# Scores from two 32 bit parts: the two heads of a pair in two 64-row halves, one PSUM bank for each score tile

## The chip, the core and the metric

The kernel runs on one core of a Trainium2 chip. The core has a matrix engine (TensorE; PE in the profile, PEld for its weight loads), a vector engine (DVE), a scalar engine (ACT), GpSimd (POOL) and a queue engine (SP) that issues most DMA transfers. Matmuls take their operands from SBUF and write to PSUM, which has eight banks; a bank holds 128 x 512 numbers of 32 bits. The engines run side by side and wait for each other on semaphores; each works through its own instructions in order.

The metric is the time of one execution on the device in microseconds, as the median of several runs.

## The reference

A block of a transformer with an attention that also has a compressive memory, 2048 positions, width 512, 32 heads of 16, and a feed-forward layer of width 1792; its input is modulated by a condition vector. The sequence is cut into four segments of 512. Cut to what matters here, the attention of a segment and head is

```python
logits = jnp.einsum("bhqd,bhkd->bhqk", qs, ks) * scale + mask     # causal
p = _softmax(logits, axis=-1)
a_dot = jnp.einsum("bhqk,bhkd->bhqd", p, vs)
o = g * a_mem + (1.0 - g) * a_dot
```

with `q = x @ wq` and so on, and `a_mem` read from the sums of earlier segments. Then come `o @ wo`, a residual, a layer norm, and the feed-forward layer with GELU. All of it is wanted at 32 bit accuracy, so the kernel splits operands of matmuls into parts and adds the products of the parts.

## The kernel before

**Stages.** The first is the projections: for each segment, layer norm, transposes, q, k, v (`proj`, `v_rows`), and the memory. The second is the attention loop with the output projection, the residual and the second layer norm woven in. The third is the feed-forward layer. In the trace they lie at about 0 to 180 us, 180 to 470 us and from there to the end.

**q and k in three parts.** `proj` (L483) makes a 128 x 512 tile of q or k in PSUM for eight heads. ACT rounds it to bfloat16 (the first part), DVE subtracts (`r1`, L497), ACT rounds the rest (second part, L508), and POOL subtracts again (third part, L509). `store` (L477) writes the parts to DRAM tiles QD and KD, which have six copies: for every product of parts that is wanted there is one place c, with one part of q in QD and one part of k in KD (`TERMS`, L162). Since a head has 16 numbers, six places make 96 rows. `load_stacks` (L172) brings the 96 rows of four heads back as `qst` and `kst` tiles of 128 x 4 x 512; one matmul over 96 rows then gives the score of a head to the accuracy of six products.

**Units of the loop.** Q counts groups of four heads within a segment (32 in all), P pairs of heads (64; P = 2Q and 2Q + 1). There are four pairs of stack tiles (`NK`). Two kinds of work make the softmax:

- S (`s_part`, L619) computes scores with query rows on the partitions, for a block i of 128 queries against the 128 (i + 1) keys that it may see, so 512, 384, 256 or 128 columns. DVE takes the negated maximum of each row: `masked_max` (L611) adds the causal mask and reduces in one instruction; for some blocks of 128 columns (`PRM['m']`: block 0 of each pair with Q below 14) a matmul adds the mask in PSUM and one `s_max` reduces both heads. S of pair P + 4 runs while T of pair P does (`LEAD`).
- T (`st_part`, L699) computes the transposed scores, key rows on the partitions, for a block j of 128 keys against 512 - 128 j queries. Three more rows (96 to 98) of the stacks hold the maxima, cut into three bfloat16 parts in `qst` against ones in `kst`, so that the matmul of 99 rows also subtracts the maximum (`st_mm`, L691). ACT takes the exponential into `pt` tiles, and POOL zeroes what the mask forbids (`causal`).

**The way of the maxima.** `m_rows` (POOL) cuts them into parts, `m_put` (PE) transposes them by a matmul with an identity into the bank of the pv tile, ACT copies them to `ms`, and `m_send` moves them by DMA into rows 96 to 98 of `qst`; the DMA is issued by SP for Q below 13 and by ACT from there on.

**The rest of the loop.** `pv_part` (L724) multiplies the exponentials of the four heads of Q with V, 32 columns for each head, so four column strips of the array; a column of ones in V gives the denominator. Then come the division (`den`, `rb_in`, `mix`) through DRAM tiles, and the output projection (`wo_part`, L815: three matmuls of 512 columns).

**The order.** It is written out by hand. The string `ORDER` is run once for each Q: `S1` is part 1 of S, `T2` part 2 of T (a token's first occurrence is for pair 2Q, its second for 2Q + 1), and `c0` to `c19` are positions at which other work is put, by numbers in `PRM`: work at 20Q + n runs at cn of Q's own turn. So `'pv'` puts the first part of pv of Q (key block 0) at 20Q + 31, which is c11 of the turn of Q + 1, and the others at c16 to c18; `'mrows'`, `'mput'` and `'msl'` place the way of the maxima; `'stacks'` (-65) places `load_stacks` at c15 four turns ahead; `'wo'` places two wo parts in a turn. Six PSUM banks (`att`) are handed out in turn to S and T; one bank is for pv and one (`mm`) for wo.

Of the kernel before, what the change touches and what calls it, by code (L numbers as in the profile page):

```python
# [25 lines left out]
ORDER = ('S1 c0 T2 T3 T2 c1 S2 c2 S3 T3 S3 c3 c4 c5 T5 S0 c6 c7 T0 c8 c9 '  # L26
         'T1 T4 S2 c10 c11 T5 S1 c12 T4 S0 c13 T0 c14 T1 c15 c16 c17 c18 c19')
# [3 lines left out]
 'mrows': -26,  # L31
 'mput': [-19, -17],
# [14 lines left out]
 'wo': [[20 * i + o for i in range(8) for o in (2, 5)]] * 2 + [[20 * i + o for i in range(4) for o in (2, 5, 8, 14)]],  # L47
# [54 lines left out]
def block_kernel(ctx: ExitStack, tc: tile.TileContext, x, wq, wk, wv, wo, betaq, betam,  # L102
# [9 lines left out]
    identb = per.tile([128, 128], BF16, name="identb")  # L112
# [59 lines left out]
    def load_stacks(Q):  # L172
        s, g, t = Q // 8, (Q // 2) % 4, Q % 2
        for st, dd in ((kst[Q % NK], KD), (qst[Q % NK], QD)):
            sp.dma_start(st[:96], dd[s][g].rearrange("c r e n -> (c r) e n")[:, 4 * t:4 * t + 4, :])
# [7 lines left out]
    v.tensor_copy(identb, ident)  # L183
# [18 lines left out]
    with ExitStack() as pa:  # L202
# [274 lines left out]
        def store(parts, nm, dd):  # L477
            rows = dd.rearrange("c r e n -> (r e) c n")
            for t, c in zip(parts, TERMS[nm]):
                d = rows[:, c]  # L480
                sp.dma_start(d, t.unsqueeze(1).to_broadcast([128, d.shape[1], 512]))

        def proj(s, nm, g):  # L483
# [7 lines left out]
            parts = [sa.tile([128, 512], BF16, tag=f"qk{i}", bufs=3, name=f"{nm}{i}{s}_{g}") for i in range(3)]  # L491
            r1 = sa.tile([128, 512], F32, tag="qkr", bufs=2, name=f"{nm}r{s}_{g}")
# [4 lines left out]
            v.tensor_tensor(out=r1, in0=ps, in1=parts[0], op=ALU.subtract)  # L497
# [10 lines left out]
            act.activation(parts[1], r1, AF.Copy)  # L508
            pool.tensor_tensor(out=parts[2], in0=r1, in1=parts[1], op=ALU.subtract)  # L509
# [74 lines left out]
    with ExitStack() as pb:  # L584
# [8 lines left out]
        nmt = [sb.tile([128, 8, 16], F32, name=f"nm{i}", bufs=1) for i in range(4)]  # L593
        for t in nmt:
            v.memset(t[:, 3:], 0.0)
# [838 lines left out]
```

## Time and profile before

| what | before |
| --- | --- |
| median of 3 runs | 785.87 us (785.84 to 789.34) |
| span of the profiled execution, first to last instruction | 783.4 us |
| the profiled execution's own time | not given apart from its span |
| PE busy | 767.0 us, 98% |
| DVE busy | 557.4 us, 71% |
| ACT busy | 470.6 us, 60% |
| granted TensorE clock | 1.000 |

In a view that groups instructions, a row names line, engine, operation, output <- inputs, shapes and count; after the first bar stand the busy time in us and the mean length of one in ns, after the second the engine's idle time ahead of them in us and who ended it. A timeline row has start and length in us. A stretch has its bounds, its length, and the busy time of PE, PEld, DVE, ACT and POOL, then the granted clock, the DMA engines' mean share and GB/s. Matmuls are pipelined: a length includes the time until the last result is written, so busy PE isn't PE at its peak.

### The profile page before, as it was taken

How to read it: one execution, taken by the hardware profiler on the slowest of the kernel's cores; microseconds unless marked ns; L12 is line 12 of the kernel's file. 1: busy time of each engine (PE TensorE's matmuls, PEld its weight loads, DVE VectorE, ACT ScalarE, POOL GpSimd, SP SyncE). 2: the span in 40 equal slices, each digit the busy share in tenths (PEclk: the TensorE clock that was granted, in tenths of full speed). 3: DMA queues.
4: the chain of work that ended last, by engine and by line, in shares of the span. 5: the costliest groups of instructions: out<-in, count | busy, mean ns of one | idle time of the engine just before them, and what ended most of it. 6: DMA issues, size and time to landing. Idle time of an engine off the chain costs nothing.

```text
span 783.4 us, 14172 instructions
## 1 busy us (share of the span) xinstructions
PE 767.0 (98%) x4549; PEld 529.0 (68%) x4549; DVE 557.4 (71%) x1540; ACT 470.6 (60%) x910; POOL 315.1 (40%) x535
## 2 busy tenths in 40 slices
PE   9999999999999999999999899999999999999998
PEld 4877776877444444455455457788878888888887
DVE  6687677548988888888987798868569764432424
ACT  4465546364888877777778676667644446652221
POOL 1256467261468556665795671243000404300000
PEclk9999999999999999999999999999999999999999
DMA  9596956487465586777677755595676624545543
GB/s 340 182 314 218 312 177 225 160 265 266 137 181 171 163 216 196 214 208 237 183 192 222 206 158 155 187 313 180 202 233 208 191 95 162 172 148 165 173 127 115
DMA packets 108819, 156.09 MB, mean 199 GB/s; under 512 B 16325, under 2 KB 55621, under 8 KB 108745
## 3 DMA queue, kind: packets, MB, share of 16 engines
q1 hardware_dynamic: 106911, 153.39, 62.4%
q10 hardware_dynamic: 1833, 1.81, 0.7%
q8 instruction: 35, 0.57, 0.3%
q14 instruction: 40, 0.32, 0.1%
HBM read 93.95 MB, written 60.83 MB: 198 GB/s over the span
## 4 chain that ended last, share of the span: by engine, by line
PE 48%; DVE 5%; DMA 5%; ACT 3%; issue 2%; POOL 2%; ACTq 0%; DVEq 0%; POOLq 0%
PE bx L1081 8%; PE bx L1351 5%; PE bv L1081 5%; PE by L1351 4%; PE bv L1351 4%; PE att L693 4%; PE pv L733 4%; PE att L606 4%; PE mm L821 3%; DMA qst<-ms 3%; PE spare L1351 2%; PE by L1081 2%; PE mm L1351 1%; ACT pt L708 1%; DMA s<-GD 1%
## 5 line engine op out<-in xcount | busy, mean ns | idle before, releaser
L613 DVE CUSTOM_DVE_ANT_0 dump<-att,maskb 128x384 bf16<-128x384 f32 (+1 forms) x456 | 208.3, 511 | 36.4 <-PE att L606 16.7
L708 ACT ACTIVATE pt<-att 128x384 f32<-128x384 f32 (+1 forms) x256 | 126.0, 545 | 33.7 <-PE att L693 16.6
L696 POOL TENSOR_SCALAR_AFFINE_SELECT pt<-pt 128x256 f32<-128x256 f32 x256 | 104.1, 422 | 68.4 <-ACT pt L708 55.7
L693 PE MATMUL att<-qst,kst 99*128 99x256 bf16 (+3 forms) x512 | 107.7, 300 | 4.2 <-DMA qst<-ms 1.8
L606 PE MATMUL att<-kst,qst 96*128 96x384 bf16 (+1 forms) x456 | 104.2, 310 | 0.8 <-DVE nm L613 0.7
L693 PEld LDWEIGHTS <-kst 99*128 99x128 bf16 x512 | 44.6, 97 | 72.6 <-issue 39.6
L865 POOL TENSOR_TENSOR wb<-wa 128x256 f32<-128x256 f32 x24 | 19.7, 821 | 153.1 <-DMA wa<-in_w 84.4
L733 PE MATMUL pv<-pt,V 128*32 128x512 f32 (+1 forms) x992 | 79.6, 439 | 0.0
L719 ACT ACTIVATE pt<-att 128x256 f32<-128x256 f32 (+1 forms) x128 | 62.4, 493 | 13.8 <-PE att L693 13.6
L136 DVE TENSOR_TENSOR gl<-s,gh 128x512 fp32r<-128x512 f32 x34 | 24.0, 707 | 42.4 <-ACT gh L133 42.4
L733 PEld LDWEIGHTS pv<-pt,V 128*32 128x32 f32 x992 | 25.9, 109 | 36.3 <-issue 30.5
L606 PEld LDWEIGHTS <-qst 96*128 96x128 bf16 x456 | 36.8, 98 | 19.2 <-issue 13.7
L133 ACT ACTIVATE gh<-s 128x512 fp32r<-128x512 f32 x34 | 21.3, 628 | 47.1 <-PE spare L1351 17.6
L1086 ACT ACTIVATE s<-s,b1t 128x512 f32<-128x512 f32 x42 | 30.3, 721 | 21.6 <-DVE s L1090 21.6
L1090 DVE TENSOR_TENSOR s<-bv,s 128x512 f32<-128x512 f32 x28 | 19.2, 687 | 30.4 <-PE bv L1081 21.2
L613 DVE DVE_READ_ACCUMULATOR2_ANT nm<- 128x1 f32 x456 | 37.7, 83 | 0.0
L509 POOL TENSOR_TENSOR q<-qr,q 128x512 bf16<-128x512 f32 x16 | 18.7, 1166 | 28.1 <-ACT q L508 27.9
L136 DVE TENSOR_TENSOR w1ml<-s,w1mh 128x512 fp32r<-128x512 f32 x18 | 13.0, 720 | 21.9 <-ACT w1mh L133 21.9
L500 POOL TENSOR_SCALAR qp<-qp 128x512 f32<-128x512 f32 x12 | 18.7, 1562 | 24.2 <-ACT qp L495 24.2
L661 POOL TENSOR_TENSOR nm<-nm 128x16 f32<-128x16 f32 x64 | 13.9, 217 | 34.3 <-DVE nm L613 31.2
L133 ACT ACTIVATE w1mh<-s 128x512 fp32r<-128x512 f32 x18 | 11.3, 628 | 25.9 <-PE spare L1351 11.6
L313 PE MATMUL q<-Ahl,wqh 128*128 128x512 f32 x64 | 26.0, 406 | 0.3 <-DVE Ahl L136 0.2
(362 smaller groups left out, 2043.5 us busy)
## 6 DMA issues: line engine op xcount, KB each, us to landing
GD<-s SPq DMA_DIRECT2D x56, 256.0 KB
s<-GD SPq DMA_DIRECT2D x52, 256.0 KB
kst<-KD SPq DMA_DIRECT2D x32, 384.0 KB
qst<-QD SPq DMA_DIRECT2D x32, 384.0 KB
TD<-ts SPq DMA_DIRECT2D x32, 256.0 KB
xt<-X2D SPq DMA_DIRECT2D x28, 256.0 KB
wa<-in_w SPq DMA_DIRECT2D x28, 256.0 KB
QD<-q SPq DMA_DIRECT2D x16, 384.0 KB
```

The source lines that it names most:

```text
L133: act.activation(hi, src, AF.Copy)
L136: lo_eng.tensor_tensor(out=lo, in0=src, in1=hi.bitcast(F32), op=ALU.subtract)
L606: pe.matmul(ps, q_of(P, h, i), k_of(P, h, 128 * (i + 1)), start=True, stop=True)
L613: v.tensor_tensor_reduce(out=dump[n_dump[0] % 2][:, :n], in0=src, in1=maskb[:, 512 - n:], scale=-1.0, scalar=-4 * NEG, op0=ALU.add, op1=AL ...
L693: pe.matmul(ps, k[:99, e, 128 * j:128 * j + 128], q[:99, e, 128 * j:512], start=True, stop=True)
L696: pool.affine_select(out=t, in_=t, pattern=pattern, compare_op=ALU.is_ge, fill=0.0, base=0, channel_multiplier=-1)
L708: act.activation(pt[:, h, :], ps[:, :n], AF.Exp, scale=0.25)
L719: act.activation(pt, pv_, AF.Exp, scale=0.25)
L733: pe.matmul(ps[32 * c:32 * c + 32, lo:hi], V[4 * s + j][:, VW * hd:VW * hd + 32], pt[:, c % 2, lo - o:hi - o], start=start, stop=stop)
L1081: pe.matmul(ps, a[:, i, k, :], b[k], start=start and k == 0 and c == 0, stop=k == 1 and c == 2, skip_group_check=not start)
L1086: act.activation(dst, src, AF.Gelu_apprx_tanh, bias=b1t[:, f:f + 1])
L1351: pe.matmul(ps, a[:, c], w[:, lo:hi], start=(f == 0 and i == 0), stop=(last and i == 2))
```

## The change

q and k are cut into two parts of 32 bits (the type that TensorE takes as fp32r), not three of bfloat16; ACT's second rounding and POOL's subtraction go. Three products of parts are kept instead of six, so a head needs 48 rows. The two heads of a pair then lie one above the other: head 0 in rows 0 to 47 and head 1 in rows 64 to 111 of the stack tiles, which are 128 x 2 x 512 numbers of 32 bits. The maxima are cut into two parts in rows 48 and 49 of each half, and T's matmuls have 50 rows.

S and T are now units of one head and one bank. Unit a is the block of 512 columns, b that of 384, c the blocks of 256 and 128 together in one bank. In `ORDER`, `Sa0` is unit a of S for head 0 of the first pair of the turn, `Tc3` unit c of T for head 1 of the second. Units of the two halves follow each other in turn. All maxima are masked maxima; the matmul that added the mask goes. The `pt` tiles are one for each unit, with three buffers for a and four for b and c.

`m_rows`, `m_put` and the wo parts get other positions, and every `m_send` is two transfers from SP. `load_stacks` is four transfers instead of two.

The core of the diff:

```diff
-ORDER = ('S1 c0 T2 T3 T2 c1 S2 c2 S3 T3 S3 c3 c4 c5 T5 S0 c6 c7 T0 c8 c9 '
-         'T1 T4 S2 c10 c11 T5 S1 c12 T4 S0 c13 T0 c14 T1 c15 c16 c17 c18 c19')
+ORDER = ('Sa0 Ta1 c0 Ta0 Sa1 c1 c2 Sb0 Tb1 c3 Tb0 Sb1 c4 c5 Sc0 Tc1 c6 Tc0 Sc1 c7 '
+         'Sa2 Ta3 c8 c9 Ta2 Sa3 c10 c11 Sb2 Tb3 c12 Tb2 Sb3 c13 Sc2 Tc3 c14 Tc2 Sc3 c15 c16 c17 c18 c19')
...
- 'mrows': -26,
- 'mput': [-19, -17],
+ 'mrows': -21,
+ 'mput': [-16, -15],
...
- 'wo': [[20 * i + o for i in range(8) for o in (2, 5)]] * 2 + [[20 * i + o for i in range(4) for o in (2, 5, 8, 14)]],
+ 'wo': [[20 * i + o for i in range(8) for o in (4, 11)]] * 2 + [[20 * i + o for i in range(4) for o in (4, 7, 11, 18)]],
...
-    QD = [[dram.tile([6, 16, 8, 512], BF16, name=f"QD{s}_{g}") for g in range(4)] for s in range(NSEG)]
-    KD = [[dram.tile([6, 16, 8, 512], BF16, name=f"KD{s}_{g}") for g in range(4)] for s in range(NSEG)]
-    TERMS = {"q": (slice(0, 3), slice(4, 6), slice(3, 4)), "k": (slice(2, 5), slice(0, 6, 5), slice(1, 2))}
+    QD = [[dram.tile([3, 16, 8, 512], F32, name=f"QD{s}_{g}") for g in range(4)] for s in range(NSEG)]
+    KD = [[dram.tile([3, 16, 8, 512], F32, name=f"KD{s}_{g}") for g in range(4)] for s in range(NSEG)]
+    TERMS = {"q": (slice(0, 3, 2), slice(1, 2)), "k": (slice(0, 2), slice(2, 3))}
...
-            d[i] = (pl or wmp).tile([128, 4, 512], BF16, **a)
-        act.activation(kst[i][96:].rearrange("p e n -> p (e n)"), one[96:].to_broadcast([32, 2048]), AF.Copy)
+            d[i] = (pl or wmp).tile([128, 2, 512], F32, **a)
+        for r in (32, 96):
+            act.activation(kst[i][r:r + 32].rearrange("p e n -> p (e n)").bitcast(F32R), one[r:r + 32].to_broadcast([32, 1024]), AF.Copy)
...
-            sp.dma_start(st[:96], dd[s][g].rearrange("c r e n -> (c r) e n")[:, 4 * t:4 * t + 4, :])
+            for h in range(2):
+                sp.dma_start(st[64 * h:64 * h + 48], dd[s][g].rearrange("c r e n -> (c r) e n")[:, 4 * t + h:4 * t + 4:2, :])
...
-            parts = [sa.tile([128, 512], BF16, tag=f"qk{i}", bufs=3, name=f"{nm}{i}{s}_{g}") for i in range(3)]
-            r1 = sa.tile([128, 512], F32, tag="qkr", bufs=2, name=f"{nm}r{s}_{g}")
+            parts = [sa.tile([128, 512], F32R, tag=f"qk{i}", bufs=3, name=f"{nm}{i}{s}_{g}") for i in range(2)]
...
-            v.tensor_tensor(out=r1, in0=ps, in1=parts[0], op=ALU.subtract)
+            v.tensor_tensor(out=parts[1], in0=ps, in1=parts[0].bitcast(F32), op=ALU.subtract)
...
-            act.activation(parts[1], r1, AF.Copy)
-            pool.tensor_tensor(out=parts[2], in0=r1, in1=parts[1], op=ALU.subtract)
...
+        def s_unit(P, z, h):
             Q, p = P // 2, P % 2
             if Q not in nms:
                 nms[Q] = nmt[Q % len(nmt)]
+            ps = bank("att")
+            o = 0
+            for i in ((3,), (2,), (1, 0))["abc".index(z)]:
                 n = 128 * (i + 1)
+                q, k = stack(qst, P, h, 48), stack(kst, P, h, 48)
+                pe.matmul(ps[:, o:o + n], q[:, 128 * i:128 * i + 128], k[:, :n], start=True, stop=True)
+                masked_max(nms[Q][:, h, p, i:i + 1], ps[:, o:o + n], n)
+                o += n
+
+        def stack(st, P, h, rows):
+            return st[P // 2 % NK][64 * h:64 * h + rows, P % 2].bitcast(F32R)
...
+            n, r = nms.pop(Q), nmr[Q % len(nmr)]
+            n = n.rearrange("q h p i -> q h (p i)")
+            hl = r[:, :32].rearrange("q (h c n) -> q h c n", h=2, c=2)
+            pool.tensor_copy(hl[:, :, 0], n)
+            pool.tensor_tensor(out=hl[:, :, 1], in0=n, in1=hl[:, :, 0].bitcast(F32), op=ALU.subtract)
+            nss[Q] = r
...
-            pe.matmul(ps[:, :128], top(ns.rearrange("q c n -> q (c n)")), identb, start=True, stop=True)
-            ms = sb.tile([48, 128], BF16, tag="ms", bufs=2, name=f"ms{Q}")
-            copy(PRM["mse"], ms, ps[:48, :128])
+            pe.matmul(ps[:, :128], nss.pop(Q), identr, start=True, stop=True)
+            ms = sb.tile([32, 128], F32, tag="ms", bufs=2, name=f"ms{Q}")
+            copy(PRM["mse"], ms, ps[:32, :128])
...
-            (sp if Q < PRM["msa"] else act).dma_start(qst[Q % NK][96:99], mss.pop(Q))
+            ms = mss.pop(Q)
+            for h in range(2):
+                sp.dma_start(qst[Q % NK][64 * h + 48:64 * h + 50], ms[16 * h:16 * h + 16])
...
+        def t_unit(P, z, h):
             ps = bank("att")
+            js = ((0,), (1,), (3, 2))["abc".index(z)]
+            m = (512, 384, 384)["abc".index(z)]
+            both = (P, z) in pth
+            if not both:
+                pth[P, z] = late[0].tile([128, 2, m], F32, tag=f"pt{z}", bufs=3 + (z != "a"), name=f"pt{z}{P}")
+            pt = pth[P, z]
+            o = 0
+            q, k = stack(qst, P, h, 50), stack(kst, P, h, 50)
+            for j in js:
                 n = 512 - 128 * j
+                pe.matmul(ps[:, o:o + n], k[:, 128 * j:128 * j + 128], q[:, 128 * j:], start=True, stop=True)
+                pts[P, j] = pt[:, :, o:o + n]
+                o += n
+            act.activation(pt[:, h, :], ps[:, :m], AF.Exp, scale=0.25)
+            if z == "c":
+                causal(pt[:, h, :256].rearrange("q (a b) -> q a b", b=128), [[0, 2], [1, 128]])
+            elif both:
                 causal(pt[:, :, 0:128], [[0, 2], [1, 128]])
```

More of the change, by code (lines that the diff above doesn't have):

```diff
@@ L603, in bank @@
             return banks[n][turn[n] % len(banks[n])]
-        def s_mm(ps, P, h, i):
-            pe.matmul(ps, q_of(P, h, i), k_of(P, h, 128 * (i + 1)), start=True, stop=True)
         dump = [sb.tile([128, 512], BF16, name=f"dump{i}", bufs=1) for i in range(2)]
@@ L649, in q_of @@
-        def q_of(P, h, i):
-            return qst[P // 2 % NK][:96, 2 * (P % 2) + h, 128 * i:128 * i + 128]
-        def k_of(P, h, n):
-            return kst[P // 2 % NK][:96, 2 * (P % 2) + h, 0:n]
-        def top(t):
-            return t.bitcast(BF16).rearrange("q (n two) -> q n two", two=2)[:, :, 1]
-        def m_rows(Q):
-            n = nms.pop(Q)
-            for c in range(2):
-                pool.tensor_tensor(out=n[:, c + 1], in0=n[:, c], in1=top(n[:, c]), op=ALU.subtract)
-            nss[Q] = n
+                q, k = stack(qst, P, h, 48), stack(kst, P, h, 48)
```

74 lines of the change are left out of this document (12 added, 62 removed).

## The prediction

> **What bounds the kernel now.** I read the page first, then busy time by stretch, then the timeline of the attention loop, then the groups by form, and last the waits.
>
> ```profile
> span 783.4 us, 14172 instructions
> ...
> PE 767.0 (98%) x4549; PEld 529.0 (68%) x4549; DVE 557.4 (71%) x1540; ACT 470.6 (60%) x910; POOL 315.1 (40%) x535
> ```
>
> PE works nearly all the time, but 98% is a mean over three stages: projections, attention loop, feed-forward. The diff touches the first two. So the second view is busy time by stretch (columns: stretch, its length, then busy us of PE, PEld, DVE, ACT, POOL).
>
> ```profile
> 180.00:196.60 16.60, 16.60 (x89) 11.60 (x88) 14.64 (x58) 7.11 (x9) 1.60 (x3) 1.00 0.73 239
> 196.60:281.30 84.70, 81.74 (x708) 39.96 (x706) 75.67 (x300) 72.15 (x161) 55.77 (x126) 1.00 0.58 169
> 281.30:394.80 113.50, 111.42 (x919) 56.09 (x920) 97.67 (x431) 86.13 (x189) 71.07 (x152) 1.00 0.72 206
> 394.80:452.00 57.20, 54.06 (x428) 29.05 (x426) 45.70 (x203) 41.80 (x90) 39.93 (x72) 1.00 0.72 205
> 452.00:470.00 18.00, 17.86 (x149) 9.08 (x147) 17.00 (x34) 13.61 (x30) 13.72 (x23) 1.00 0.59 166
> ```
>
> I cut the stretches at the first T matmuls of Q 0, 11 and 24, so they hold 11, 13 and 6 iterations; ahead of them two iterations run S alone, behind them two run T alone. The loop runs from 180 to 470. PE is full in it, but DVE is close behind: 75.67 of 84.70, 97.67 of 113.50, 17.00 of 18.00. That second bound decides the size of any gain. Next, PE's own order in one iteration (start, length, instruction; a length includes the pipeline's tail, so cost is read from start to start).
>
> ```profile
> 327.69 1.07 PE L733 MATMUL pv<-pt,V 128*32 128x512 f32 x8
> 328.69 0.28 PE L693 MATMUL att<-qst,kst 99*128 99x128 bf16 x2
> 328.81 0.49 PE L606 MATMUL att<-kst,qst 96*128 96x384 bf16 x2
> 329.14 0.38 PE L693 MATMUL att<-qst,kst 99*128 99x256 bf16 x2
> 329.36 0.60 PE L606 MATMUL att<-kst,qst 96*128 96x512 bf16 x2
> 329.79 0.59 PE L693 MATMUL att<-qst,kst 99*128 99x512 bf16 x2
> 330.32 1.50 PE L733 MATMUL pv<-pt,V 128*32 128x384 f32 x24
> 331.75 0.50 PE L606 MATMUL att<-kst,qst 96*128 96x384 bf16 x2
> ...
> 333.44 0.48 PE L821 MATMUL mm<-woh,oh 128*128 128x512 f32 x1
> ...
> 334.23 0.29 PE L606 MATMUL att<-kst,qst 96*128 96x128 bf16 x2
> ```
>
> Score matmuls stream back to back: two of 512 columns take 0.43 us, of 384 0.33, of 256 0.22, of 128 0.12, together 1.10. An iteration has two pairs of heads, each with S and T, so 4 x 1.10 = 4.4 us. The pv groups take 1.00 us (512 columns) and 1.43 us (768 columns), so 0.43 us is the price of 256 columns and about 0.14 us of each group is fixed. One wo part takes 0.79 us, two 1.58. With 4.4 + 2.43 an iteration without wo has 6.8 us of PE, one with wo 8.4. Then DVE's groups from 205 to 485 (count, busy us, mean ns, idle before).
>
> ```profile
> L613 DVE CUSTOM_DVE_ANT_0 dump<-att,maskb 128x512 bf16<-128x512 f32 x116 | 75.1, 685 | 5.5 <-PE att L606 5.5
> L613 DVE CUSTOM_DVE_ANT_0 dump<-att,maskb 128x384 bf16<-128x384 f32 x114 | 59.1, 555 | 22.9 <-PE att L606 10.3 <-POOL nm L661 10.0 <-POOL pt L696 1.6
> L613 DVE CUSTOM_DVE_ANT_0 dump<-att,maskb 128x256 bf16<-128x256 f32 x115 | 44.1, 420 | 6.9 <-ACT pt L708 3.5 <-ACT ms L127 3.0 <-issue 0.3
> L613 DVE DVE_READ_ACCUMULATOR2_ANT nm<- 128x1 f32 x417 | 34.5, 83 | 0.0
> L613 DVE CUSTOM_DVE_ANT_0 dump<-att,maskb 128x128 bf16<-128x128 f32 x72 | 17.5, 288 | 0.1
> L617 DVE TENSOR_REDUCE nm<-att 128x2 f32<-128x256 f32 x22 | 8.3, 418 | 0.0
> ```
>
> Busy time by count, a masked maximum costs 0.65, 0.52, 0.38 and 0.24 us for 512, 384, 256 and 128 columns (a little of each lies beside the next). These are most of DVE's 75.67 / 11 = 6.9 us per iteration in the second stretch and 97.67 / 13 = 7.5 in the third. DVE idles mostly for PE, and nothing in the change makes its maxima cheaper.
>
> **The change, part by part.**
>
> *Score matmuls.* They have 48 or 50 rows instead of 96 or 99, and the two heads of a pair lie in rows 0 and 64. Consecutive units (Sa0, Ta1) then use different halves of the array and different banks. No row of this trace shows two row halves at work together. The nearest is pv: eight instructions of 512 columns in 1.00 us, where eight at the 0.21 us of a score matmul would take 1.7; its four column strips work side by side. Bounds for the 4.4 us: 2.2 if halves overlap fully, 4.4 plus slower loads if not at all. These rows tell of the loads:
>
> ```profile
> L693 PEld LDWEIGHTS <-kst 99*128 99x128 bf16 x512 | 44.6, 97 | 72.6 <-issue 39.6 <-DMA qst<-ms 4.7
> ...
> L313 PEld LDWEIGHTS q<-Ahh,wql 128*128 128x128 f32 x64 | 12.0, 188 | 2.1
> ```
>
> ```profile
> 54.63 3.62 PE L413 MATMUL mp<-V,pk 128*128 128x128 f32 x31
> ```
>
> A 32 bit load takes 188 ns instead of 97. Thirty-one matmuls of 128 columns, each with a 32 bit load, follow each other in 3.62 / 31 = 0.12 us, so such a load can be started every 0.12 us. A matmul of 512 columns hides one, a matmul of 128 doesn't. With halves overlapping, S of two heads costs 0.21 + 0.16 + 0.12 + 0.12 = 0.61, T the same, and the 4.4 becomes 4 x 0.61 = 2.4 (2.8 if a 32 bit matmul of 128 columns takes four times as long per column; no row has one). If the loads of both halves share one path, 32 x 0.12 = 3.8. I take 2.4, because pv's strips, the nearest row, overlap with their loads. PE also leaves the halves once more per iteration (the c4 group of maximum rows and wo; c11 lies beside pv): 0.14 us, pv's fixed part. New PE sum: 2.4 + 2.43 + 0.14 = 5.0 without wo, 6.6 with it. Both lie below DVE, which is late next.
>
> [...]
>
> *DVE.* 28 pairs (two for each Q below 14) had a mask matmul and one reduction of 8.3 / 22 = 0.38 us; now they have two maxima of 128, 0.49 us: 28 x 0.11 = 3 us more on what now bounds. DVE's idle time doesn't vanish: six banks alternate, so at most three S units wait for DVE, some 1.6 us of its work. Pv's second group takes 1.43 us and the first, with a wo part, 1.8; the next unit needs about 0.3 more. I estimate 0.25 us of idle at the second group everywhere, and at the first where a wo part stands in it.
>
> *ACT.* Exponentials keep their columns; two of 384 replace one of 512 and one of 256:
>
> ```profile
> L708 ACT ACTIVATE pt<-att 128x384 f32<-128x384 f32 x121 | 52.6, 492 | 20.2 <-PE att L606 13.6 <-PE att L693 6.5
> L719 ACT ACTIVATE pt<-att 128x512 f32<-128x512 f32 x62 | 37.4, 603 | 4.6 <-PE att L693 4.5
> L719 ACT ACTIVATE pt<-att 128x256 f32<-128x256 f32 x62 | 23.7, 383 | 9.2 <-PE att L693 9.2
> ```
>
> 984 against 986 ns, nothing. But a wait is added. Tiles pta have three buffers, and Ta3 now stands ahead of c11, where pv releases the oldest; four would be live. So ACT's exponential of Ta3 waits for pv's first group, with Ta2's and all later ones queued behind it. PE doesn't wait for it to reach pv. Price: pv's 1.0 us less one exponential, some 0.6 us of ACT. ACT's 86.13 / 13 = 6.6 us per iteration becomes 7.2, still below the new period; in the second stretch it is 72.15 / 11 + 0.6 = 7.2, as long as DVE's share there, and where it isn't covered it costs up to 0.6 per iteration.
>
> *Maximum rows and stacks.* The rows leave at c5 instead of c2, as two transfers on SP; those of Q from 13 on were ACT's. SP issues them behind the stacks (c15 of the iteration before), pv's loads (c16) and its store (c2); behind them come the denominators' loads (c8). The stacks become four transfers instead of two.
>
> ```profile
> 325.31 7.39 DMA qst<-ms
> ```
>
> ```profile
> L675 SPq DMA_DIRECT2D qst<-ms x13: 723/777/837, 192.6 to 283.1; - x13
> ```
>
> ```profile
> 330.42 0.33 SPq L175 DMA_DIRECT2D kst<-KD  x1
> ```
>
> Extra issue time on SP is 0.78 + 2 x 0.33 = 1.4 us per iteration, hidden because SP otherwise waits; uncovered it would delay the maximum rows by 0.78. This transfer took over 7 us from its issue, and yet the load row above shows only 4.7 us of waits for such. From c5 to the next T lie 8 of 12 S units: the period of 8.0 less 2 x (0.65 + 0.52) for the first four is 5.7 us. The transfer queues behind those issued before it, and three positions later less is left of these. I charge 2 us in all. POOL's two steps on the maxima and ACT's copy stay.
>
> *Projections.* One ACT copy and one POOL subtraction go per projection; bytes stored and loaded stay the same.
>
> ```profile
> 100.00:150.00 50.00, 49.75 (x249) 37.55 (x248) 33.97 (x55) 26.20 (x47) 30.93 (x25) 1.00 0.60 197
> ```
>
> PE has 49.75 of 50.00 there, so both hide behind PE: 0 to 1 us, I take 0.
>
> **Sum**, by the five loop rows, as DVE busy + extra + idle. 16.60 (no T, no pv): 14.64 + 0.4 = 15.1, -1.5. 84.70 with 11 iterations: 75.67 + 22 x 0.11 + 11 x 0.25 = 80.8, -3.9. 113.50 with 13: 97.67 + 0.3 + 13 x 0.5 = 104.5, -9.0. 57.20 with 6: 45.70 + 3.0 = 48.7, but PE idles there now too (54.06 of 57.20) and POOL has longer work, so of the 8.5 I take 5. 18.00: DVE has 17.00, so -0.5. Together -19.9, and with 2 for late transfers -17.9. The profiled span of 783.4 becomes 765.5. The page gives the span alone; the median of the runs, 785.87, is 2.5 above it, which I add: 768. The feed-forward behind the loop is PE's own, so a gain in the loop isn't given back.
>
> **Rivals.**
> - *Loads share one path* (3.8 instead of 2.4): PE with wo is 3.8 + 2.43 + 1.58 + 0.14 = 8.0, as much as DVE's 7.5 + 0.5, so each waits for the other at times: 0.3 us in 19 iterations, 774. The load rows leave this open.
> - *The halves don't overlap*: slower. 32 bit matmuls stream one after another as now, and the 8 of 128 columns grow from 0.06 to 0.12 (+0.5), with 0.14 for the group; the mask matmuls that go give back some 0.2 before Q 11. It decides as soon as PE's sum passes the present one. +0.64 in 19 iterations and +0.44 in 11 make +17, 803; with 128 columns at four times the column time (0.21) another 8 x 0.09, 825. Against it speaks pv's overlap of strips. [...]
> - *Maximum rows come late*: 7.39 + 0.78 for the second issue less 5.7 is 2.5 us of PE wait; three S units cover 1.6. If every iteration from Q 10 on pays 0.9, 20 x 0.9 = 18: 786, no change. The few waits of now speak against it.
> - *DVE never idles*: the 2.75 + 6.5 + 3.0 of idle time go, 756.
>
> **Chances.** Forecast 0.54 (own range 758 to 774), one load path 0.10, DVE full 0.12, rows late 0.11, no overlap 0.13. A measurement of this kernel tells some 0.5% (4 us) from no change. Faster by more: 0.54 + 0.10 + 0.12 = 0.76; within: 0.11; slower: 0.13. The range 753 to 789 leaves out no overlap and the tails.
>
> **What would show it.** Right: in the profile after, score matmuls of both halves start within some 0.05 us of each other, equal pv groups stand some 7.3 us apart before Q 11 and some 8 after, DVE is over 92% busy from 200 to 430, PE shows idle time in front of score matmuls that DVE ends, and feed-forward lasts as long as now. Wrong: score units one after another, a PE wait on the maximum rows in most iterations, or ACT idle by over 1 us in front of Ta3 with DVE waiting behind it.

## The result and the profile after

The change makes the kernel slower: 1025.38 us (median of 4 runs, 1022.69 to 1034.32) against 785.86 for the kernel before, measured beside it, a ratio of 1.3073 with a 95% interval of 1.3005 to 1.3141. Ratios below are to the kernel before too, with their 95% interval in brackets. The forecast was 768, the range 753 to 789. (Ratios here leave out disturbed executions, so one can lie a little beside the quotient of two medians.) The profiled execution took 1025.51 us, with a span of 1023.8.

From the page of the changed kernel: the span, the engines' busy time, the granted clock in 40 slices (9 is full speed, 5 is half), and two of its costliest groups.

```profile
span 1023.8 us, 14348 instructions
...
PE 920.7 (90%) x4521; PEld 600.4 (59%) x4521; DVE 577.9 (56%) x1624; ACT 453.1 (44%) x882; POOL 279.9 (27%) x503
...
PEclk9999999755565555666665658878999999999999
...
L610 DVE CUSTOM_DVE_ANT_0 dump<-att,maskb 128x512 bf16<-128x512 f32 (+3 forms) x512 | 236.9, 489 | 246.9 <-PE att L622 130.2
L622 PE MATMUL att<-kst,qst 48*128 48x512 f32 (+3 forms) x512 | 216.4, 501 | 87.6 <-DVE nm L610 87.6
```

PE's busy time rose by 154 us although its score matmuls have half the rows. All of that rise lies in the attention loop (438.0 us of PE in the five stretches below, 281.7 in those of the prediction), slices 8 to 28 of the clock row, and there TensorE ran at a clock of about 0.5 to 0.8; before, it was 1.000 throughout. And DVE and PE wait for each other: 246.9 us of idle time stand in front of the maxima, 130.2 of them for PE, and 87.6 us in front of S's matmuls, all of it for DVE.

The same five loop stretches as in the prediction, cut at the first T matmuls of Q 0, 11, 24 and 30 (columns as there):

```profile
176.70:210.80 34.10, 28.04 (x82) 17.12 (x81) 16.08 (x70) 6.88 (x9) 0.83 (x4) 0.69 0.34 107
210.80:374.50 163.70, 134.19 (x684) 64.88 (x683) 86.81 (x360) 71.67 (x160) 56.73 (x124) 0.56 0.37 88
374.50:595.00 220.50, 179.52 (x923) 87.27 (x919) 110.62 (x441) 85.49 (x189) 74.55 (x153) 0.62 0.43 106
595.00:693.50 98.50, 79.16 (x458) 38.25 (x454) 50.20 (x208) 42.99 (x93) 39.28 (x73) 0.78 0.53 133
693.50:711.00 17.50, 17.09 (x111) 8.72 (x114) 15.66 (x28) 11.46 (x26) 10.82 (x17) 0.86 0.34 106
```

All of the loss is in the loop: 534.3 us instead of 290.0. The feed-forward layer behind it takes 312.8 us, against 313.4 before. A turn takes 163.70 / 11 = 14.9 us in the second stretch, 7.7 before; the clock column is 0.56 there.

The timeline shows the start of it, while the clock is still full (0.98 from 180.7 to 183.1 us, 0.50 in the 2.9 us behind that). These are the first two units c of S, on PE and DVE (start, length, instruction, and idle time before it with what ended it):

```profile
180.73 0.38 PE L622 MATMUL att<-kst,qst 48*128 48x256 f32 x1
...
181.15 0.42 DVE L610 CUSTOM_DVE_ANT_0 dump<-att,maskb 128x256 bf16<-128x256 f32 x1 [0.26 <-PE att L622]
...
181.64 0.38 PE L622 MATMUL att<-kst,qst 48*128 48x128 f32 x2 [0.53 <-DVE nm L610]
182.00 0.29 DVE L610 CUSTOM_DVE_ANT_0 dump<-att,maskb 128x128 bf16<-128x128 f32 x1 [0.42 <-PE att L622]
...
182.69 0.54 PE L622 MATMUL att<-kst,qst 48*128 48x128 f32 x2 [0.68 <-DVE nm L610]
183.06 0.29 DVE L610 CUSTOM_DVE_ANT_0 dump<-att,maskb 128x128 bf16<-128x128 f32 x1 [0.42 <-PE att L622]
```

A unit c puts 256 columns and then 128 into one bank. In the code DVE's maximum over the 256 stands between the two matmuls. So PE writes 256 columns and waits until DVE has read them; then DVE waits for the 128. (The kernel before issued both matmuls of a shared bank ahead of both maxima; the new `s_unit` gave that order up.) The two engines take turns, and all that is queued behind the second matmul on PE, the other half's units too, waits with it: PE is busy for 1.20 of the 2.40 us from 180.7 to 183.1. In each of the 128 units c of this trace the second matmul starts 0.06 to 0.07 us after the read has ended (in the rows above at 181.64, against 181.15 + 0.42 = 181.57), although by the code it writes other columns of the bank than those that are read. The view of waits over the loop counts them (who waits for whom: us in total, times, longest):

```profile
DVE dump L610 <- PE att L622: 130.2, 204, 3.9
PEld att L622 <- DVE nm L610: 121.4, 128, 1.9
PE att L622 <- DVE nm L610: 87.6, 128, 1.6
```

128 times is once for each unit c (32 turns x 4). But 87.6 us of PE's waiting don't make 240; that the rest has to do with the clock is what the experiments have to show.

### The profile page after: what moved, and what is told of

Its sections match the earlier page's. It is cut to its first block, busy times and chain, and to the rows that moved or that the text cites. A ratio compares the mean times of both kernels' runs of the same rounds, so it can differ in the third digit from the quotient of the medians.

```text
span 1023.8 us, 14348 instructions
## 1 busy us (share of the span) xinstructions
PE 920.7 (90%) x4521; PEld 600.4 (59%) x4521; DVE 577.9 (56%) x1624; ACT 453.1 (44%) x882; POOL 279.9 (27%) x503
## 4 chain that ended last, share of the span: by engine, by line
PE 74%; DVE 10%; issue 9%; POOL 2%; DMA 2%; ACT 2%; SPq 0%; DVEq 0%; ACTq 0%
PE att L622 11%; PE pv L702 9%; PE bx L1048 7%; DVE dump L610 7%; PE att L681 5%; PE mm L790 5%; PE bx L1318 4%; PE q L315 4%; PE by L1318 4%; PE bv L1318 4%; PE bv L1048 4%; PE k L315 3%; PE v L466 3%; PE spare L1318 2%; PE by L1048 2%
## 5 line engine op out<-in xcount | busy, mean ns | idle before, releaser
L610 DVE CUSTOM_DVE_ANT_0 dump<-att,maskb 128x512 bf16<-128x512 f32 (+3 forms) x512 | 236.9, 489 | 246.9 <-PE att L622 130.2
L622 PE MATMUL att<-kst,qst 48*128 48x512 f32 (+3 forms) x512 | 216.4, 501 | 87.6 <-DVE nm L610 87.6
L622 PEld LDWEIGHTS att<-kst,qst 48*128 48x128 f32 x512 | 117.9, 262 | 182.2 <-DVE nm L610 121.4
L681 PE MATMUL att<-qst,kst 50*128 50x512 f32 (+3 forms) x512 | 165.9, 487 | 8.2 <-DVE nm L610 7.6
L684 ACT ACTIVATE pta<-att 128x512 f32<-128x512 f32 x128 | 69.4, 595 | 102.3 <-PE pv L702 48.5
L681 PEld LDWEIGHTS att<-qst,kst 50*128 50x128 f32 x512 | 89.0, 265 | 27.8 <-DVE nm L610 23.3
L684 ACT ACTIVATE ptc<-att 128x384 f32<-128x384 f32 x128 | 55.9, 488 | 90.6 <-PE att L681 73.8
L666 POOL TENSOR_SCALAR_AFFINE_SELECT ptc<-ptc 128x256 f32<-128x256 f32 x128 | 51.5, 413 | 95.9 <-ACT ptc L684 91.4
L684 ACT ACTIVATE ptb<-att 128x384 f32<-128x384 f32 x128 | 57.5, 499 | 16.8 <-PE att L681 10.5
L702 PE MATMUL pv<-pta,V 128*32 128x512 f32 x248 | 56.5, 1002 | 0.0
```

Of the source, the lines that this page charges most:

```text
L610: v.tensor_tensor_reduce(out=dump[n_dump[0] % 2][:, :n], in0=src, in1=maskb[:, 512 - n:], scale=-1.0, scalar=-4 * NEG, op0=ALU.add, op1=AL ...
L622: pe.matmul(ps[:, o:o + n], q[:, 128 * i:128 * i + 128], k[:, :n], start=True, stop=True)
L666: pool.affine_select(out=t, in_=t, pattern=pattern, compare_op=ALU.is_ge, fill=0.0, base=0, channel_multiplier=-1)
L681: pe.matmul(ps[:, o:o + n], k[:, 128 * j:128 * j + 128], q[:, 128 * j:], start=True, stop=True)
L684: act.activation(pt[:, h, :], ps[:, :m], AF.Exp, scale=0.25)
L702: pe.matmul(ps[32 * c:32 * c + 32, lo:hi], V[4 * s + j][:, VW * hd:VW * hd + 32], pt[:, c % 2, lo - o:hi - o], start=start, stop=stop)
```

## The experiments

Two theories of the loss at first. **Theory 1**: the wait in unit c is the cause, and the clock falls because PE stands still. **Theory 2**: half-height matmuls use too little of the array, and the clock falls whether PE waits or not. (The first expectation has a third, that the two halves don't work side by side; the streams of matmuls below answer it.)

**Both matmuls of unit c ahead of both maxima.** The one edit in the changed kernel:

```diff
+            maxima = []
...
-                masked_max(nms[Q][:, h, p, i:i + 1], ps[:, o:o + n], n)
+                maxima.append((nms[Q][:, h, p, i:i + 1], ps[:, o:o + n], n))
                 o += n
+            for x in maxima:
+                masked_max(*x)
```

> The changed kernel with one edit: in unit c of S both matmuls (256 and 128 columns) are issued ahead of the two maxima, so the second matmul no longer waits until DVE has read the first from the same bank. Theory 1 (this wait starts the loss, and the low clock only follows from PE's idle time): granted clock 1.000, time 755 to 775 us, PE hardly idle for DVE ahead of 128-column score matmuls. Theory 2 (matmuls on 48 of 128 rows are too little activity for the clock by themselves): the clock stays below 0.9 and the time above 850. Theory 3 (the two halves don't run side by side): clock 1.000, but 800 to 825.

Measured: 865.16 us (859.91 to 867.58), ratio 1.1029 [1.0976, 1.1083], mean clock 0.909. So the order of two matmuls and a maximum is worth 160 us of the 240. None of the three expected results came: the time is above 850, as by theory 2, but the clock isn't below 0.9. Neither theory alone is enough. Turns 2 to 10 (no wo parts) and 13 to 18 (two wo parts each) of this kernel, by stretch:

```profile
213.20:315.80 102.60, 99.11 (x589) 47.03 (x585) 68.94 (x296) 60.05 (x133) 49.20 (x104) 0.60 0.52 123
339.80:396.90 57.10, 49.91 (x432) 26.25 (x428) 47.37 (x201) 38.30 (x87) 32.63 (x70) 1.00 0.76 194
```

Without the wait PE is busy for 99.11 of 102.60 us in the first stretch, and still its clock is 0.60 and a turn takes 11.4 us. With wo parts, which are matmuls of full height, the clock is 1.00 and a turn takes 9.5 us, although it holds more work and PE idles more. That speaks for theory 2 in what was left.

**The wait alone, in the kernel before.** All blocks of 128 columns get masked maxima, and in the bank that two heads share the second head's matmul stands behind the first one's maximum; rows and parts stay:

```diff
- 'm': [[0, 1, 0, 1], [1, 1, 1, 1]],
+ 'm': [[1, 1, 1, 1], [1, 1, 1, 1]],
...
-                    for h in range(2):
```

> The kernel before with all maxima masked, and in the tiles that both heads share (256 and 128 columns) head 1's matmul issued behind head 0's maximum: the same wait of PE for DVE, four times in an iteration, with matmuls of 96 rows and without halves. Theory 1: each wait leaves PE idle some 0.7 us, so 2.5 to 3 us per iteration in 32 iterations, 860 to 890 us if the clock stays at 1.000; over 950 with a clock below 0.9 if PE's idle time alone lowers it. Theory 2: the clock stays at 1.000 here, since the matmuls use 96 rows.

Measured: 902.22 us in one execution, mean clock 0.953, which neither theory had forecast. Turns 3 to 10 (no wo parts), then turn 20 (wo parts, clock full):

```profile
237.00:339.40 102.40, 82.40 (x522) 33.04 (x520) 60.50 (x264) 55.26 (x120) 45.48 (x95) 0.77 0.38 110
...
448.70:460.20 11.50, 9.20 (x73) 4.46 (x71) 7.89 (x35) 7.01 (x16) 6.02 (x13) 1.00 0.63 171
```

Where the clock is full a turn takes 11.50 us; in the third stretch of the kernel before it took 113.50 / 13 = 8.73. So a wait costs (11.50 - 8.73) / 4 = 0.7 us, as expected. In turns without wo the clock falls here too, with 96 rows, and turns 3 to 10 take 12.8 us each; only turn 2 kept 1.00 and took 10.30. So waits lower the clock as well; rows are not the only way to it.

**Full-height work in the wait.** Behind the first matmul of each unit c, in turns 0 to 10 of the changed kernel, four matmuls of 128 rows and 512 columns whose result nobody reads (called fillers below):

```diff
+                if i == 1 and 2 <= Q <= 12:
+                    for _ in range(4):
+                        pe.matmul(mm, maskb[:, :128], maskb, start=True, stop=True)
```

> The changed kernel with the wait left in, and four idle-time matmuls of 128 rows and 512 columns (bfloat16, into the bank that wo doesn't use yet) behind the first matmul of unit c in the turns 0 to 10; their results are not used. If the low clock is a large part of the loss and comes from PE's idle time: clock near 1.000 in these turns, a turn of 10 to 11.5 us instead of 15.2, the whole some 45 us shorter than the changed kernel. If the wait alone makes up the loss, the turns stay near 15 us or grow.

Measured: 1003.02 us in one execution. Turns 2 to 10, and 12 to 24 without fillers:

```profile
239.40:350.30 110.90, 103.34 (x724) 46.63 (x729) 70.11 (x296) 58.16 (x133) 49.11 (x102) 1.00 0.49 114
365.20:588.70 223.50, 182.91 (x929) 88.27 (x925) 110.56 (x443) 85.77 (x190) 81.19 (x155) 0.60 0.44 106
```

More work makes the turns shorter: 110.90 / 9 = 12.3 us instead of 15.3 (137.50 / 9 in the changed kernel), at a clock of 1.00 instead of 0.57. The gain of 22 us was half of the 45 expected; that the fillers' own time stands in the wait is a likely reason, not shown. So at full clock a turn with the wait is at most 12.3 us, and at least 3 us of the 15.3 are the clock's.

**Streams of matmuls by themselves.** A kernel that computes nothing of the block: matmuls one behind the other into eight banks, nothing that reads them, with stretches of full-height matmuls between.

```python
for i in range(200): rows(i // 2, 64 * (i % 2), 512, qq, kk)   # 48 rows, the two halves in turn
whole(50)                                                       # 128 rows, 512 columns
for i in range(120): rows(i, 0, 512, qq, kk)                    # 48 rows, one half only
```

> No part of the block is computed: streams of matmuls alone, without any wait for another engine, each between streams of 128 rows x 512 columns in 32 bits. Halves overlapping (rows 0 and 64 in turn, 48 rows, own banks): 200 matmuls of 512 columns take 21 to 24 us, of 256 columns 11 to 13 us (24 us if the loads of both halves share one path), of 128 columns 11 to 13 us (21 us if such a 32 bit matmul takes four times as long per column); no overlap: 43 to 46 us for 512 columns. Theory 1: the clock stays at 1.000 in all streams. Theory 2: it falls to one half in the streams of 48 rows, the one on a single half above all.

Timeline of PE (one row for a whole stream), then busy time by stretch (the granted clock is the third number from the right):

```profile
4.26 24.31 PE L53 MATMUL bank<-kk,qq 128*128 128x512 f32 x100 [4.26 <-DVE qq L39]
28.50 22.98 PE L58 MATMUL bank<-kk,qq 48*128 48x512 f32 x200
...
62.97 46.75 PE L58 MATMUL bank<-kk,qq 48*128 48x512 f32 x120
...
122.98 12.25 PE L58 MATMUL bank<-kk,qq 48*128 48x256 f32 x200
...
147.17 18.62 PE L58 MATMUL bank<-kk,qq 48*128 48x128 f32 x200
...
180.33 22.44 PE L74 MATMUL bank<-kk,qq 128*128 128x128 f32 x200
```

```profile
28.50:51.40 22.90, 22.90 (x201) 19.88 (x200) 0.00 (x0) 0.00 (x0) 1.00 0.00 1
62.90:68.60 5.70, 5.70 (x26) 4.56 (x26) 0.00 (x0) 0.00 (x0) 1.00 0.00 0
68.60:109.60 41.00, 41.00 (x97) 31.03 (x95) 0.00 (x0) 0.00 (x0) 0.50 0.00 0
...
150.50:165.70 15.20, 15.20 (x146) 15.10 (x142) 0.00 (x0) 0.00 (x0) 0.50 0.01 1
180.40:202.60 22.20, 22.20 (x201) 22.20 (x200) 0.00 (x0) 0.00 (x0) 1.00 0.00 1
```

Three things are to be seen. The halves do work together: 200 matmuls of 48 rows take 22.98 us, so a pair takes 0.23 us, as long as one of full height (the 50 behind them take 11.63 us). Loads and short matmuls don't stop them: 256 columns cost 12.25 / 200 = 0.06 us each with a 32 bit load for each. And a single half, with PE busy in every microsecond and no gap, falls to half clock after 5.7 us. Of the 200 halves with 128 columns some 54 run in the first 3.3 us, 0.06 us each; then the clock is 0.50 and the other 146 take 15.20 us, so their stream takes 18.62 us and not the 11 to 13 expected; full-height matmuls with the same 128 columns, one only every 22.44 / 200 = 0.112 us, keep 1.00. That is theory 2 without any wait: in these streams the clock goes with how much of the array is in use, not with whether PE has something to do.

**Fillers where no wo part stands.** To the kernel with the mended unit c, three fillers at c4 and at c11 in turns 0 to 11, where later turns have their wo parts:

```diff
+        for Q in range(12):
+            for d in (4, 11):
+                ap(20 * Q + d, fill, 3)
```

> x1 with three matmuls of 128 rows and 512 columns (bfloat16, results unused, into the bank that wo doesn't use yet) at c4 and at c11 of the turns 0 to 11, where a wo part stands in later turns. Theory: in these turns the array is too little in use, since a score matmul fills 48 of 128 rows and pv alone stands beside it; wo parts keep the clock up in turns 13 to 18 of x1. Then the clock is 1.000 in turns 1 to 11, a turn falls from 11.5 to 9.0 to 9.8 us and the whole to 835 to 845 us. Rival: PE's added work costs as much as the clock brings, 860 or more.

Measured: 842.51 us in one execution. Turns 2 to 10 take 82.6 / 9 = 9.2 us at a clock of 1.00 (11.4 at 0.60 without fillers), as expected. Turns 13, 21, 23 to 25 and 28 stayed slow, at clocks of 0.64 to 0.78, although they have wo parts; in turn 23 PE stood 2.5 us for POOL.

**Pv's first part at c7 instead of c11**, so that the exponential of Ta3 needn't wait for it (`'pv': [[27, 0, 0, 512], ...`):

> x5 with the first part of pv at c7 instead of c11, so ahead of Sa2 and Ta3. Theory: ACT's exponential of Ta3 waits for that part of pv because unit a has three buffers, and PE's long group at c11 leaves DVE without tiles; with pv at c7 the ACT wait goes and PE's groups are shorter: 0.5 to 1 us less per turn, 812 to 828 us. Rival: the wait is hidden behind DVE's work, as the prediction had it: within 5 us of x5.

Measured: 833.29 us in one execution, and in a second launch of the same kernel 831.15 (824.80 to 839.06, 4 runs), ratio 1.0562 [1.0487, 1.0638]. The turns became 0.4 us shorter, 79.10 / 9 = 8.8 instead of 9.2; less than the 0.5 to 1 expected. The four executions of the second launch lie up to 14 us apart, so a single execution of these kernels tells the whole time only that closely; the turns by stretch are the firmer reading. What was expected of the second launch (it speaks of a run that follows below), and its first case came:

> The kernel of the run with pv's first part at c7 once more, timed in rounds, since one execution cannot tell 833 from the 804 to 821 that four executions of the run with the cuts at c15 gave. If the move of the cuts is worth what it seemed, 828 to 836 with a clock near 0.97; if that one execution was an outlier, 805 to 815 with a clock near 0.99.

**All other PE work moved apart**, pv's parts to c7, c12, c16 and c17, and the second wo part or filler to c14, to feed DVE more evenly (the base is the kernel with fillers at c4 and c11):

```diff
- 'pv': [[31, 0, 0, 512], [36, 1, 128, 512], [37, 2, 256, 512], [38, 3, 384, 512]],
+ 'pv': [[27, 0, 0, 512], [32, 1, 128, 512], [36, 2, 256, 512], [37, 3, 384, 512]],
...
- 'wo': [[20 * i + o for i in range(8) for o in (4, 11)]] * 2 + [[20 * i + o for i in range(4) for o in (4, 7, 11, 18)]],
+ 'wo': [[20 * i + o for i in range(8) for o in (4, 14)]] * 2 + [[20 * i + o for i in range(4) for o in (4, 7, 11, 18)]],
...
-            for d in (4, 11):
+            for d in (4, 14):
```

> x5 with pv in four places (c7, c12, c16, c17) and the second wo part, or the matmuls in its place, at c14: PE's work that is not scores comes in groups of at most 1.0 us. Theory: DVE idles because at most three score tiles wait for it while PE is in such a group, so shorter groups bring the turn near DVE's own 7.5 us: 785 to 810 us. Rival: each further change between halves and the whole array costs more than the shorter groups bring: as x6 or slower.

Measured: 863.33 us in one execution, 21 more than with fillers at c4 and c11. That is slower, as the rival had it, but the rival's reason (changes between halves and whole array) isn't shown. Turns 2 and 3, then turn 7, then turn 9, by stretch:

```profile
214.10:231.50 17.40, 16.46 (x146) 7.96 (x142) 13.93 (x65) 12.54 (x29) 8.38 (x22) 1.00 0.67 154
258.40:272.50 14.10, 12.64 (x77) 5.33 (x73) 8.63 (x36) 7.09 (x16) 6.65 (x15) 0.64 0.41 102
281.20:290.80 9.60, 8.14 (x74) 3.94 (x71) 8.37 (x35) 6.50 (x15) 4.72 (x12) 1.00 0.57 140
```

Turns 2 and 3 take 8.7 us each at full clock; turn 7 has the same PE work and takes 14.1 at a clock of 0.64, and turn 11 does the same. But turn 7 also has a longer wait: PE stands 1.46 us in it for DVE, where the longest wait in turns 2 and 3 is 0.47. Turns 9 and 11 have the same 1.46 us, and turn 9 kept 1.00. So turns with the same work and the same wait can keep the clock or lose it; a mean over a turn isn't what decides. Whether the place of the full-height work or the longer wait let it fall here isn't shown.

**POOL's cutting of the maxima at c15 instead of c19.** The view of waits of the kernel with pv at c7, turns 21 to 24, has these rows:

```profile
PEld pv L642 <- POOL nmr L637: 5.3, 2, 3.4
PE pv L642 <- POOL nmr L637: 4.8, 2, 3.2
```

PE stood up to 3.2 us for the cut maxima, since POOL was at the layer norm and the output projection, which the new position c19 puts ahead of them (before, it was c14); in front of the cut at 418.91 us these took 2.09 and 1.26 us. The edit is one number (`'mrows': -25`).

> The kernel of the run with pv's first part at c7, with POOL's cutting of the maxima at c15 instead of c19, so that it stands ahead of POOL's work on the output projection and the second layer norm. In the run before, PE waited 3.2 and 1.6 us for these cuts in turns 23 and 24, and DVE idled 4.5 us behind. Theory 1 (part of the late turns' length is this queue): turns 23 to 25 lose those 5 us and what the low clock adds behind them; 820 to 828. Theory 2 (POOL is simply full there, 8 to 11 us per turn): what is moved ahead delays the output projection as much, 831 to 837.

Measured: 809.08 us (803.67 to 820.86), ratio 1.0293 [1.0249, 1.0338]. That is 22 us less than the 831, below the range of either theory and more than the waits themselves; the clock of these turns comes back with them. Turns 21 to 24 with the cuts at c19 (the run with pv at c7), then at c15:

```profile
391.50:440.40 48.90, 40.82 (x284) 20.89 (x283) 33.60 (x141) 26.51 (x59) 29.91 (x53) 0.83 0.62 150
390.70:428.70 38.00, 34.48 (x286) 18.71 (x285) 33.65 (x143) 26.76 (x60) 28.96 (x50) 1.00 0.83 202
```

**Fillers in the late turns too**, three into pv's bank ahead of its first part in turns 12, 13 and 20 to 29, on top of the cuts at c15:

```diff
+        def fill_pv(n):
+            ps = bank("pv")
+            for _ in range(n):
+                pe.matmul(ps, maskb[:, :128], maskb, start=True, stop=True)
...
+            if Q in (11, 12, *range(19, 29)):
+                ap(20 * Q + 27, fill_pv, 3)
```

> The kernel of the run with the cuts at c15, with three full-height matmuls of 512 columns into the pv bank just ahead of pv's first part in turns 12, 13 and 20 to 29. They cost some 0.65 us of PE each turn where the clock is full, 12 x 0.65 = 8 us at most. Theory 1 (little use of the array is what lowers the clock in turns 13, 21, 23 to 25 and 28): these six turns go from 13 to 15 us to 9.5 to 10.5, about 25 us less, 800 to 812. Theory 2 (the waits for other engines lower it, whatever runs between): no turn changes its clock, and the fillers only cost, 3 to 10 us above the run with the cuts at c15.

Measured: 813.91 us (811.92 to 817.27), ratio 1.0382 [1.0347, 1.0417], mean clock 0.994. With the cuts at c15 there was little clock left to win, and the fillers cost 5 us on the whole, the size that theory 2 gave; its reason, that no turn changes its clock, isn't tested by that. The run tells how the loop looks at nearly full clock. Its five stretches (the view and its cuts as above):

```profile
178.30:195.70 17.40, 17.40 (x82) 11.22 (x81) 14.17 (x63) 6.88 (x9) 0.42 (x2) 1.00 0.58 186
195.70:293.00 97.30, 91.66 (x752) 45.61 (x751) 79.46 (x368) 70.25 (x160) 55.75 (x124) 0.96 0.62 147
293.00:416.60 123.60, 114.61 (x944) 60.59 (x941) 101.23 (x442) 83.02 (x189) 72.15 (x149) 1.00 0.78 189
416.60:485.20 68.60, 63.69 (x476) 33.11 (x472) 48.41 (x208) 42.57 (x93) 42.30 (x79) 0.98 0.71 187
485.20:501.80 16.60, 15.20 (x111) 7.62 (x114) 16.19 (x29) 11.39 (x26) 11.56 (x17) 1.00 0.58 163
```

**No fillers, and two instead of three.** Both are the kernel with the cuts at c15, once with its fillers' lines taken out (so that three edits of the changed kernel remain) and once with `fill, 2` in the place of `fill, 3`.

> The kernel of the run with the cuts at c15 without the fillers of turns 0 to 11: the changed kernel with three edits (both score matmuls of unit c ahead of its maxima, pv's first part at c7, the cuts at c15). Theory 1 (a turn without wo parts uses the array too little, so its clock falls): turns 2 to 11 go from 8.7 to about 11 us at a clock of 0.6 to 0.7, some 22 us in all, 825 to 835. Theory 2 (the waits that the two moves took away were what lowered the clock in these turns): they take 7.5 to 8.3 us at 1.00, 797 to 806.

> The kernel of the run with the cuts at c15 with two fillers at each place instead of three. A filler of 512 columns costs 0.23 us of PE, so where the clock holds, turns 2 to 11 are up to 0.46 us shorter: 803 to 807. If the clock needs the third (0.46 us of full-height work in a turn of 8.5), turns 2 to 11 fall to a clock of 0.6 to 0.9 and take 9.5 to 11 us: 815 to 830.

Measured without fillers: 821.16 us (815.09 to 830.00), ratio 1.0422 [1.0331, 1.0512]; with two: 809.24 (805.23 to 826.46), ratio 1.0293 [1.0227, 1.0359], the same as with three. Both lie between the ranges of their theories. Without fillers both theories were right in part, in one and the same execution. Turns 5 and 6, then 7 to 9, then 14 to 17 with wo parts:

```profile
244.50:261.00 16.50, 14.60 (x136) 7.72 (x132) 14.32 (x67) 13.72 (x31) 12.66 (x25) 1.00 0.64 164
261.00:294.10 33.10, 31.57 (x199) 15.83 (x195) 21.51 (x99) 19.79 (x44) 16.13 (x37) 0.60 0.56 134
330.00:366.10 36.10, 33.78 (x287) 18.25 (x284) 30.41 (x135) 25.36 (x58) 21.66 (x46) 1.00 0.85 200
```

The same kind of turn takes 8.25 us at a clock of 1.00 and 11.0 at 0.60. This kernel lies on the border. Two fillers don't lead safely past it: in the profiled execution of that kernel (826.46 us) turns 2 and 3 ran at half clock, 13.3 us each, and turns 4 to 10 at 1.00, 8.44 each:

```profile
214.70:241.30 26.60, 25.65 (x140) 11.84 (x138) 14.12 (x64) 13.59 (x29) 8.38 (x21) 0.51 0.45 98
241.30:300.40 59.10, 54.66 (x480) 27.80 (x483) 50.50 (x231) 46.38 (x104) 39.42 (x81) 1.00 0.67 166
```

## Why the prediction was wrong

From the forecast of 768 to the 1025 measured are 257 us. The runs took off 160 with the order in unit c, 23 with fillers, 11 with pv at c7 and 22 with POOL's cuts, down to 809; the 41 left are DVE's idle time in part. The 23 and the 11 both rest on one execution of the kernel with fillers at c4 and c11, and in the last kernel the fillers are worth 12 (821 against 809).

- **Unit c, "Score matmuls" and "DVE": 160 us.** I gave the units different banks and halves and let consecutive ones overlap. I didn't follow the order of matmul, maximum, matmul inside one unit, where both matmuls go to one bank. "Six banks alternate, so at most three S units wait for DVE" holds between units only. The 0.7 us that one such wait costs at full clock, four times in 32 turns, would have made 90 us; what it does to the clock is the rest (argued by difference; the fillers in the wait show 3 us a turn of it).
- **The clock.** The sum has no term for it: I read 1.000 in the profile before and took it as given. The change halves the rows in use, and the waits thin them out further. With the waits a turn without wo ran at 0.57, without them at 0.60 where it fell. Showing that wait and clock are two causes took both the kernel before with the wait (0.77) and the stream without waits (0.50).
- **"POOL's two steps on the maxima stay": 22 us.** They stay, but they moved from c14 to c19, past POOL's work on the output projection and the layer norm. I checked the queue of SP for this move and not POOL's, and it was POOL's that made PE wait up to 3.2 us for the cut maxima.
- **DVE's idle time, mis-sized: about 27 us.** By the rows without fillers DVE idles (16.50 - 14.32) / 2 = 1.09 us per turn without wo, where the estimate was 0.25, and (36.10 - 30.41) / 4 = 1.42 with wo, where it was 0.5. Twelve turns of the one kind and 19 of the other make 0.84 x 12 + 0.92 x 19 = 27.6 us. The timeline of the same kernel around pv's first group, which stands at c7 there and not at c11, shows both wrong steps:

```profile
247.37 0.42 DVE L610 CUSTOM_DVE_ANT_0 dump<-att,maskb 128x256 bf16<-128x256 f32 x1
...
247.45 1.07 PE L705 MATMUL pv<-pta,V 128*32 128x512 f32 x8
...
248.45 0.50 PE L623 MATMUL att<-kst,qst 48*128 48x512 f32 x1
...
248.53 0.08 DVE L610 DVE_READ_ACCUMULATOR2_ANT nm<- 128x1 f32 x1
...
249.08 0.69 DVE L610 CUSTOM_DVE_ANT_0 dump<-att,maskb 128x512 bf16<-128x512 f32 x1 [0.47 <-issue]
```

  When pv starts, two units c wait for DVE, 248.61 - 247.37 = 1.24 us of work and not 1.6. And from pv's end to the next maximum it is 249.08 - 248.45 = 0.63 us and not 0.3. So the first group leaves DVE idle for 0.47 us even where no wo part stands in it.
- **ACT's wait for pv: not covered.** It was found (Ta3 ahead of c11) and priced at 0.6 us of ACT, hidden. In the changed kernel ACT stood 48.5 us for pv in front of its `pta` exponentials (group L684 of the profile's page), and pv at c7 instead made a turn 0.4 us shorter. So part of it wasn't hidden; how much isn't shown, since that move also makes PE's long group shorter.

What was right: the halves overlap with their loads, and 128 columns of 32 bits cost no fourfold time (0.06 us for 256 columns, and for 128 while the clock is full; the 2.4 us). DVE's busy time is nearly as summed: 259.5 us over the five stretches with late fillers, against 250.7 + 3.1 = 253.8 by the prediction's terms without its idle time. The feed-forward keeps its length. That DVE is the bound is right only in part: in the rows without fillers it is 87% and 84% busy at full clock, not over 92% as the prediction would have it, and PE 88% and 94%; at times each waits for the other. The transfers of the maxima hardly mattered: in the loop of the kernel without fillers PE waited for them 2.2 us in all. Of the rivals, the one that ended slower was "the halves don't overlap", and that one is refuted; slower came by a mechanism that I didn't list. Even at nearly full clock and with the four edits (809 us) the change stays 2.9% slower than the kernel before. In the kernel without fillers a turn at full clock takes 8.25 us without wo and 9.03 with it, where before they took 7.7 and 8.7 by the stretches of the prediction. So PE's shorter scores brought nothing here; that DVE's idle time behind pv is why is argued from the rows above. Splitting that remainder further, or a turn order that keeps DVE fed without wo parts, wasn't tried beyond the spread above.

## What to carry to other kernels

When several matmuls share a PSUM bank, issue all of them before the first instruction that reads it: one maximum between two matmuls cost 0.7 us at full clock, and the 128 of them 160 us in the whole kernel with what followed. Before halving the rows of PE's matmuls, ask how much of the array is left in use, and count a lower clock as a rival with its own price, even where the profile before shows 1.000: here a single half alone fell to 0.50 after 5.7 us, and the turns without wo ran at 0.57. Before counting a gain on an engine that is then no longer the bound, ask whether the next one has enough queued to bridge each long block of the first: here DVE idled 1.09 us in a turn of 8.25 where 0.25 was expected, and the turn was no shorter than the 7.7 us before.

## What the runs showed of the hardware

The granted clock fell with PE busy all the time: in the stream of a single half PE is busy for 41.00 of 41.00 us at 0.50. An estimate of the array's use, as columns streamed times share of rows, with 0.23 us for 512 columns at full height: a single half of 48 rows uses 37% and falls to half clock (0.50); 128 columns at full height, one each 22.44 / 200 = 0.112 us where they stream for 0.057, use 51% and keep 1.00. In the loop, pv's 1280 columns at full height stream for 2.15 us (0.43 for 256) and the scores count 4 x 1280 x 2 x 0.23 / 512 x 49 / 128 = 1.76, together 3.9. Without wo or fillers that is 3.9 / 8.25 = 47%, and the clock goes up and down (1.00 in turns 5 and 6, 0.60 in turns 7 to 9); with six fillers (6 x 0.23 more) it is 5.3 / 9.2 = 58%, and turns 2 to 11 kept it in all five profiled executions with six (turn 1 fell in each, to 0.55 to 0.72).

Between these the same estimate doesn't decide. Four fillers make 4.8 / 8.44 = 57%, and turns 2 and 3 fell (0.51) where turns 4 to 10 kept 1.00. The spread order has 5.3 / 9.6 = 55% in a turn with the longer wait, and two of three such turns fell (0.64 and 0.63). The kernel before with the wait has (4.4 x 98 / 128 + 2.15) / 10.30 = 54%; turn 2 kept 1.00, and turns 3 to 10 fell (0.77 over them). So in these runs the border lies at about half of the array's use by this estimate, with both outcomes between 47% and 57%. Over what stretch of time the use is taken, and whether the way up has the same border as the way down, is open.
